# Turning the dilated heads two tokens at a time

## The chip, the core and the metric

The kernel runs on one NeuronCore of a Trainium2 chip. The metric is the device time of one execution in microseconds. Every execution starts with the inputs in HBM and ends when the last output tile has landed there.

The core has TensorE for matmuls (PE in the profile; PEld is its loading of weights), VectorE (DVE), ScalarE (ACT), GpSimd (POOL, which issues the loads here) and SyncE (SP, which issues the stores here). Each runs its own program in order and waits for the others on semaphores. Matmuls write PSUM; DVE and ACT copy results from there to SBUF.

## The reference

Sliding-window attention, of which half of the heads are dilated, and then a soft mixture of experts in which every expert sees four weighted means of all tokens.

```python
# q, k, v: (batch 8, heads 8, seq 576, head_dim 64), float32
scores = q @ k.T / 8
rel = pos[:, None] - pos[None, :]
mask_plain = (rel >= 0) & (rel < 32)                      # heads 0 to 3
mask_dil = (rel >= 0) & (rel < 128) & (rel % 4 == 0)      # heads 4 to 7
attn = softmax(where(mask, scores, -1e9));  out = attn @ v
x = out.transpose(0, 2, 1, 3).reshape(4608, 512)          # tokens x (heads * dim)

logits = x @ phi                                          # phi: 512 x 32 (8 experts x 4 slots)
d = softmax(logits over the 4608 tokens);   slot_input = d.T @ x
slot_out[e] = relu(slot_input[e] @ w1[e]) @ w2[e]         # w1[e]: 512x1024, w2[e]: 1024x512
c = softmax(logits over the 32 slots);      result = c @ slot_out   # 4608 x 512, float32
```

A dilated head sees, from a token, the 32 tokens before it with the same remainder mod 4. If the tokens are put in an order in which all of one remainder lie side by side, a dilated head has the same band of 32 as a plain one.

## The kernel before

**Units.** Attention is done in 8 units (`NU`). Unit u handles batches 2(u // 2) and 2(u // 2) + 1, and one type of heads, `ty = u % 2`: even units the four plain heads, odd units the four dilated ones. So a pair of units finishes two batches. `load_unit` (L387) brings q, k and v of a unit into one of three staging buffers `stg`, converted to bf16 by the DMA: 96 partitions (3 tensors x 2 heads `h01` x 8 pieces of 72 tokens x 2 batches `bpar`), and on the free axis two heads `x` x 72 tokens x 64 dims.

**Steps of a unit**, each an `op` with the engine that it runs on:

- `st_T` (turning; PE L515, ACT L532), four times, j = 0 to 3: PE transposes slices of `stg`, ACT copies them from PSUM to `TT`, where the head dims lie on the partitions. One transpose takes one token slot c of one head x: 96 partitions x 64 columns in, 64 x 96 out. The two heads x go to the partition halves 0 to 63 and 64 to 127. Each call makes 2 x 9 x 2 = 36 transposes. For odd units j is the remainder mod 4, so that `TT` holds the tokens in order of remainder.
- `st_S` (PE L550, ACT L557, DVE L565), six times: scores of four blocks of 96 queries against 128 keys (`QB` 96 plus a `HALO` of 32), for both partition halves; exp on ACT to `PT`; the mask times it on DVE.
- `st_V` (PE L575, DVE L580), four times: V turned back to tokens on partitions, with a column of ones: `VN`.
- `st_P` (PE L603, DVE L612 and L614), four times: P times V; division by the row sums gives `XB`, tokens on partitions.
- `st_X` (PE L631, then L640 on DVE or L641 on ACT), four times: `XB` turned by six transposes of 96 x 128, and one copy of 128 x 576 out of PSUM to `XT`. The planner gives a copy to DVE or to ACT, whichever is free first in its account.
- `st_L`, after each odd unit, for both of its batches: logits of a batch out of `XT` of the plain (c = 0, 1) and dilated heads (c = 2, 3), eight matmuls (PE L660); exp on ACT to `expT` (L665), in natural token order; two small copies `expX` (DVE L672); the logits turned to tokens on partitions, in the order of each head type (PE L692, DVE L696); and the sum over tokens of d.T @ x into `psA` (PE L705).

**Order.** All ops are handed to a planner in the kernel (`Prog.schedule`). Each has a cost, a due time (`due`, a `PACE` of 13.1 us a unit) and a mode of the PE array (`mode`: "f" full, "h" column halves, "r" row halves, "c" column quarters); a change of mode is booked at 0.11 us. The planner simulates the engines with these costs and writes the order of each engine's program; so a changed cost can change the order everywhere. From 125 us on in its own account it puts dummy matmuls (`filler`, L889) where it sees PE wait.

**Loads.** POOL issues all loads in program order. `load_unit(u + 3)` waits until unit u is turned, as it takes its staging buffer. The 16 weight matrices of the experts (1 MB each in bf16) go to a buffer of their own (`WD`, seven), into the staging buffers of units 5, 6 and 7 once those are turned (six), and into `TT` (three), once unit 7's scores and V are read.

**The end.** After unit 7: `fold` (L752), first layer (L772), row sums (L809), hidden layer turned (L790), second layer (L830), and then the output (L869, L872, L875, stores on SP).

Of the kernel before, what the change touches and what calls it, by code (L numbers as in the profile page):

```python
# [21 lines left out]
QB = 96  # L22
# [269 lines left out]
def bass_dilated_sliding_attn__then__soft_moe_slots_kernel(  # L292
# [205 lines left out]

    def win(u, t, h01, i, bpar):

        base = (2 * t + h01) * S + QB * i - (HALO if t else 0)
        n = QB if t == 0 else 128
        return TT[:, u % 2, 2 * base + bpar:2 * (base + n - 1) + bpar + 1:2]

    def st_T(u, j):
        ty, s = u % 2, u % 3
        src = stg[0:96, s, :].rearrange("r (x c d) -> r x c d", x=2, c=CT)
        pt = tile(psum, 2)

        def pe(t):  # L510
            for a in range(2):
                for kk in range(9):
                    c = 18 * j + 9 * a + kk if ty == 0 else 4 * (9 * a + kk) + j
                    for hx in range(2):
                        i_ = t.transpose(  # L515
                            bankb2(pt, a)[64 * hx:64 * hx + 64, 96 * kk:96 * kk + 96],
                            src[:, hx, c, :], ident[0:96, 0:96])
            return i_
        op("pe", pe, r=[b_id, b_stg[s]], w=[pt], alloc=[pt], cost=0.86, mode="h",
           key=due(u, 0.5 * j))  # L520

        def ev(ac):
            sv = pair(pt)[:, :, 0:432].rearrange("p a (k w) -> p w a k", w=48)
            t32 = TT[:, u % 2, :].bitcast(F32)
            if ty == 0:
                d = t32.rearrange("p (w c) -> p w c", c=CT)[:, :, 18 * j:18 * j + 18]
                d = d.rearrange("p w (a k) -> p w a k", a=2)
            else:
                d = t32.rearrange("p (s n) -> p s n", s=6)[:, :, 144 * j:144 * j + 144]
                d = d.rearrange("p s (w a k) -> p s w a k", a=2, k=9)  # L530
                sv = sv.rearrange("p (s w) a k -> p s w a k", w=8)
            return ac.activation(d, sv, ACTF.Copy)  # L532
        op("act", ev, r=[pt], **{"w" if j == 0 else "a": [b_TT[u % 2]]}, cost=0.8,
           key=due(u, 0.8 + 0.5 * j))
# [4 lines left out]
    def st_S(u, i):  # L539
        ty = u % 2  # L540
        sc, pt = tile(psum, 2), tile(pPT)
        U[u]["p", i] = pt

        def pe(t):
            for x in range(4):
                gi = 4 * i + x
                g, blk_ = gi // 6, gi % 6
                bpar, h01 = g // 2, g % 2
                for hx in range(2):
                    i_ = t.matmul(pair(sc)[:, hx, QB * x:QB * x + QB],  # L550
                                  win(u, 1, h01, blk_, bpar)[64 * hx:64 * hx + 64],
                                  win(u, 0, h01, blk_, bpar)[64 * hx:64 * hx + 64],
                                  start=True, stop=True)
            return i_
        k0 = due(u, 4.0 + 1.3 * i)
        op("pe", pe, r=[b_TT[u % 2]], w=[sc], alloc=[sc, pt], cost=0.2, mode="r", key=k0)
        op("act", lambda ac: ac.activation(  # L557
            sbt(pt)[:, 0:768].rearrange("p (x n) -> p x n", x=2), pair(sc)[:, :, 0:384],
            ACTF.Exp, scale=SCALE), r=[sc], w=[pt], cost=0.71, key=k0 + 0.6)
        m0 = (4 * i) % 6  # L560

        def mk(dv):
            m = mask[ty][:, m0:m0 + 4, :].rearrange("p m x -> p (m x)")
            p_ = sbt(pt)[:, 0:768].rearrange("p (x n) -> p x n", x=2)
            return dv.tensor_tensor(p_, p_, m.unsqueeze(1).to_broadcast([128, 2, 384]), AluOp.mult)  # L565
        op("dve", mk, r=[b_mask[ty]], w=[pt], cost=0.47, key=k0 + 1.5)
# [18 lines left out]
    def st_P(u, g):  # L585
        bp, ty = u // 2, u % 2
        bpar, h01 = g // 2, g % 2
        b = 2 * bp + bpar
        po, rv = tile(psum, 2), tile(pRV)
        vn = U[u]["v", g]  # L590
        al = [po]
        if h01 == 0:
            XB[b, ty] = tile(pXB)
            al.append(XB[b, ty])
        xb = XB[b, ty]
        pts = {(6 * g + m) // 4: U[u]["p", (6 * g + m) // 4] for m in range(6)}

        def pe(t):
            for m in range(6):
                i, x = divmod(6 * g + m, 4)  # L600
                for hx in range(2):
                    o_ = 384 * hx + QB * x
                    i_ = t.matmul(pair(po)[:, hx, 65 * m:65 * m + 65],  # L603
                                  sbt(pts[i])[:, o_:o_ + 128],
                                  sbt(vn)[:, m, hx, 0:65], start=True, stop=True)
            return i_
        k0 = due(u, 8.5 + 2.0 * g)
        op("pe", pe, r=list(pts.values()) + [vn], w=[po], alloc=al, cost=0.41, key=k0)

        def pv():  # L610
            return pair(po)[0:QB, :, 0:390].rearrange("p x (m d) -> p x m d", d=65)
        op("dve", lambda dv: dv.reciprocal(sbt(rv)[:], pv()[:, :, :, 64]),  # L612
           r=[po], w=[rv], alloc=[rv], cost=0.15, key=k0 + 1.0)
        op("dve", lambda dv: dv.tensor_tensor(  # L614
            sbt(xb)[:].rearrange("p m (x h d) -> p h x m d", x=2, h=2)[:, h01], pv()[:, :, :, 0:64],
            sbt(rv)[:].unsqueeze(3).to_broadcast([QB, 2, 6, 64]), AluOp.mult),
           r=[po, rv], **{"w" if h01 == 0 else "a": [xb]}, cost=0.87, key=k0 + 1.2)

    def st_X(u, bpar, x):
        bp, ty = u // 2, u % 2  # L620
        b = 2 * bp + bpar
        px = tile(psum, 1)
        al = [px]
        if x == 0:
            XT[b, ty] = tile(pXT)
            al.append(XT[b, ty])
        xt, xb = XT[b, ty], XB[b, ty]

        def pe(t):
            for m in range(6):  # L630
                i_ = t.transpose(bankb(px)[:, QB * m:QB * m + QB],  # L631
                                 sbt(xb)[:, m, 128 * x:128 * x + 128], ident[0:QB, 0:QB])
            return i_
        k0 = due(u, 13.0 + 4.0 * bpar + 0.8 * x)
        op("pe", pe, r=[b_id, xb], w=[px], alloc=al, cost=0.28, key=k0)

        def ev(en):
            d, s_ = sbt(xt)[:, x, :], bankb(px)[:, 0:S]
            if en is nc.vector:
                return en.tensor_copy(d, s_)  # L640
            return en.activation(d, s_, ACTF.Copy)  # L641
        op(("dve", "act"), ev, r=[px], **{"w" if x == 0 else "a": [xt]},
           cost={"dve": 0.38, "act": 0.55}, key=k0 + 0.6)

    def st_L(b, u):
        lg = tile(psum, 2)
# [2 lines left out]
        def pe(t):  # L649
            flat = pair(lg).rearrange("p a x -> p (a x)")  # L650
            for lo, hi in ((0, 192), (192, 576)):
                for c in range(4):
                    o_ = flat[:, 320 + lo:320 + hi]
                    if c < 2:
                        rhs = sbt(x0)[:, c, lo:hi]
                    else:
                        o_ = o_.rearrange("p (i r) -> p r i", r=4)
                        rhs = sbt(x1)[:, c - 2, :].rearrange("p (r i) -> p r i", r=4)[
                            :, :, lo // 4:hi // 4]
                    i_ = t.matmul(o_, phi_pad[:, c].rearrange("p j i -> p (j i)"), rhs,  # L660
                                  start=c == 0, stop=c == 3)
            return i_
# [5 lines left out]
            cost=0.56, key=k0 + 1.3)  # L668
        for h_ in range(2):
            def cp(dv, h_=h_):  # L670
                n = expT[:, S * b:S * b + S].rearrange("p (i x y) -> p x y i", x=2, y=2)
                return dv.tensor_copy(  # L672
                    expX[:].rearrange("p (x y i) -> p x y i", x=2, y=2)[:, :, h_],
                    n[:, :, h_, 96 * (1 - h_):96 * (1 - h_) + 48])
            op("dve", cp, r=[b_expT[b]], **{"w" if h_ == 0 else "a": [b_expX]}, cost=0.15,
               key=k0 + 2.2)
# [3 lines left out]
        def pe2(t):  # L680
            nat = expT[:, S * b:S * b + S]
            for i in range(12):
# [3 lines left out]
                elif m % 3 == 1:  # L686
                    l_ = expX[:, QB * (m // 3):QB * (m // 3) + QB]
                else:
                    f_ = QB * m
                    o_ = 4 * (f_ % 144) + f_ // 144  # L690
                    l_ = nat[:, o_:o_ + 4 * 95 + 1:4]
                i_ = t.matmul(bank(pe_t)[0:128 if i < 6 else QB, 32 * i:32 * i + 32], l_, sel[:],  # L692
                              start=True, stop=True)
            return i_
        op("pe", pe2, r=[b_expT[b], b_expX, b_sel] + b_expT[b + 1:b + 2], w=[pe_t], alloc=[pe_t, et], cost=0.5, key=k0 + 2.4)
        op("dve", lambda dv: dv.tensor_copy(  # L696
            sbt(et)[:], bank(pe_t)[0:QB, 0:384].rearrange("p (i s) -> p i s", s=32)),
           r=[pe_t], w=[et], cost=0.45, key=k0 + 3.2)
# [51 lines left out]
    def pe_f(t):  # L750
# [1 line left out]
            i_ = t.matmul(bank(fo)[:, 32 * c:32 * c + 32], psA_sb[:, c::4], fold[:],  # L752
                          start=True, stop=True)
        return i_
    op("pe", pe_f, r=[b_psA, b_fold], w=[fo], alloc=[fo], cost=1.4, key=K1)
    for hi in range(2):
        op("dve", lambda vv, hi=hi: vv.tensor_copy(
            siT[:, hi, :, :, 4 * hi:4 * hi + 4],
# [183 lines left out]
```

## Time and profile before

| | |
|---|---|
| runs | 640.96, 189.43, 189.08 us; median 189.43 |
| profiled execution | 190.36 us |
| its span, first to last instruction | 188.6 us |
| mean granted TensorE clock | 0.926 |
| PE busy | 142.1 us (75%), 2872 matmuls and as many weight loads |
| DVE, ACT busy | 110.1 us (58%), 94.2 us (50%) |
| loads (software queue) | 30.94 MB written to SBUF |
| stores | 9.44 MB to HBM |
| instruction queue (q8) | 22 packets, 0.36 MB |

How to read the rows of the profile: a row of the timeline is start and length in us, engine, line of the kernel, operation, output<-inputs, tile, and count of instructions that were merged; in brackets the idle time of the engine ahead of it and what ended it. `96*64 96x96` on PE: 96 rows and 64 columns of the array in use, 96 x 96 moving elements. "issue" as a releaser: the engine waited for nothing that the profile shows. A matmul's own length includes the way through the array; what a series costs is seen from start to start. In rows of groups, the numbers behind the bar are busy us, mean ns of one, then idle us ahead of them.

### The profile page before, as it was taken

Reading aid. Unit: us, or ns where it says so; the run is one execution under the profiler, and the core shown is the slowest. Engines: PE = TensorE matmul, PEld = TensorE weight load, DVE = VectorE, ACT = ScalarE, POOL = GpSimd, SP = SyncE. Lnnn points to the kernel's source line nnn. Section 1 sums busy time; section 2 is a strip of 40 time slices with the busy share of each in tenths; the row PEclk is TensorE's granted clock in tenths of the full one; section 3 lists DMA queues with packets and bytes.
Section 4 is the critical chain, followed back from the end, with each engine's and each line's share of the span. In section 5 each row is a group of like instructions: output and inputs, shape, how many; then the busy total and the mean of one; then the engine's idle time right before and its main releaser. Section 6 shows DMA issues by size and latency. Waiting matters only on the chain.

```text
span 188.6 us, 6342 instructions
## 1 busy us (share of the span) xinstructions
PE 142.1 (75%) x2872; PEld 104.4 (55%) x2872; DVE 110.1 (58%) x256; ACT 94.2 (50%) x136; POOL 35.8 (19%) x72
## 2 busy tenths in 40 slices
PE   0028879599987878998949799887899999996000
PEld 0028668487766757776837677675664658311000
DVE  6820794496687359569528966948943130699000
ACT  2006857456675655675649476478321020699000
POOL 7980603301500420440020020010400000000000
PEclk9999999669999978999996999999699999999855
DMA  5999999999999999999999999949999950199998
GB/s 76 211 215 211 213 212 218 213 216 215 212 210 220 216 208 221 213 212 215 216 216 208 219 219 217 208 99 151 219 215 214 215 109 3 60 405 405 407 403 322
DMA packets 7898, 40.83 MB, mean 216 GB/s; under 512 B 1856, under 2 KB 1856, under 8 KB 4416
## 3 DMA queue, kind: packets, MB, share of 16 engines
q0 software_dynamic: 4752, 30.94, 79.9%
q1 hardware_dynamic: 3120, 9.50, 12.8%
q8 instruction: 22, 0.36, 0.7%
q14 instruction: 4, 0.03, 0.0%
HBM read 61.93 MB, written 9.44 MB: 378 GB/s over the span
## 4 chain that ended last, share of the span: by engine, by line
PE 50%; DVE 26%; issue 5%; DMA 5%; ACT 4%; POOL 1%; DVEq 0%; POOLq 0%
PE ps L515 13%; DVE PT L565 8%; PE ps L660 6%; DVE XB L614 6%; PE ps L631 6%; DVE WD L875 5%; DVE VN L580 5%; DMA stg<-in_v_dram 5%; PE ps L889 4%; PE ps L575 4%; PE ps L603 3%; PE ps L550 3%; PE ps L830 3%; ACT PT L557 2%; PE ps L772 2%
## 5 line engine op out<-in xcount | busy, mean ns | idle before, releaser
L532 ACT ACTIVATE TT<-ps 128x864 f32<-128x864 f32 x32 | 28.3, 894 | 30.0 <-PE ps L515 30.0
L515 PE MATMUL ps<-ident,stg 96*64 96x96 bf16 x1152 | 32.4, 215 | 14.4 <-DMA stg<-in_v_dram 12.9
L557 ACT ACTIVATE PT<-ps 128x768 bf16<-128x768 f32 x48 | 37.4, 810 | 10.0 <-PE ps L550 10.0
L515 PEld LDWEIGHTS ps<-ident,stg 96*64 96x64 bf16 x1152 | 28.3, 116 | 16.6 <-DMA stg<-in_v_dram 12.9
L614 DVE TENSOR_TENSOR XB<-ps,RV 96x768 bf16<-96x768 f32 x32 | 30.2, 945 | 0.5
L580 DVE COPY VN<-ps 128x768 bf16<-128x768 bf16 x32 | 17.6, 549 | 19.2 <-PE ps L575 19.1
L550 PE MATMUL ps<-TT 64*128 64x96 bf16 x384 | 17.9, 221 | 4.5 <-issue 2.5
L603 PE MATMUL ps<-VN,PT 128*128 128x65 bf16 x384 | 19.0, 203 | 2.8 <-DVE VN L580 1.1
L575 PE MATMUL ps<-ident,TT 128*128 128x128 bf16 x192 | 18.4, 238 | 2.3 <-issue 2.3
L603 PEld LDWEIGHTS ps<-VN,PT 128*128 128x128 bf16 x384 | 15.7, 104 | 5.3 <-DVE VN L580 1.5
L396 POOL DMA_DIRECT2D stg<-in_q_dram x16 | 8.4, 526 | 51.3 <-PE ps L515 50.5
L631 PE MATMUL ps<-ident,XB 96*128 96x96 bf16 x192 | 13.6, 214 | 5.1 <-DVE XB L614 3.0
L575 PEld LDWEIGHTS ps<-ident,TT 128*128 128x128 bf16 x192 | 12.5, 107 | 7.9 <-issue 5.3
L631 PEld LDWEIGHTS ps<-ident,XB 96*128 96x128 bf16 x192 | 10.4, 103 | 8.1 <-issue 3.7
L550 PEld LDWEIGHTS ps<-TT 64*128 64x128 bf16 x384 | 10.8, 102 | 7.2 <-ACT PT L557 1.6
L641 ACT ACTIVATE XT<-ps 128x576 bf16<-128x576 bf16 x16 | 10.4, 648 | 8.2 <-PE ps L631 8.2
L640 DVE COPY XT<-ps 128x576 bf16<-128x576 bf16 x16 | 7.3, 455 | 11.4 <-PE ps L631 11.4
L565 DVE TENSOR_TENSOR PT<-PT,mask_d 128x768 bf16<-128x768 bf16 x24 | 12.8, 535 | 0.9 <-ACT PT L557 0.5
L660 PE MATMUL ps<-XT,phi_pad 128*128 128x192 bf16 (+1 forms) x64 | 13.0, 362 | 0.0
L565 DVE TENSOR_TENSOR PT<-PT,mask_p 128x768 bf16<-128x768 bf16 x24 | 12.7, 541 | 0.0
L612 DVE RECIPROCAL RV<-ps 96x12 f32<-96x12 f32 x32 | 7.1, 223 | 7.9 <-PE ps L603 7.8
L425 POOL DMA_DIRECT2D stg<-in_moe_w_dram x6 | 3.2, 534 | 42.1 <-PE ps L515 42.1
(75 smaller groups left out, 161.5 us busy)
## 6 DMA issues: line engine op xcount, KB each, us to landing
WD<-in_moe_w_dram POOLq DMA_DIRECT2D x7, 1024.0 KB, 25.4
out_dram<-WD SPq DMA_DIRECT2D x14, 512.0 KB, 5.0
stg<-in_moe_w_dram POOLq DMA_DIRECT2D x6, 1024.0 KB, 15.2
stg<-in_q_dram POOLq DMA_DIRECT2D x16, 288.0 KB, 13.2
stg<-in_k_dram POOLq DMA_DIRECT2D x16, 288.0 KB, 14.9
stg<-in_v_dram POOLq DMA_DIRECT2D x16, 288.0 KB, 17.5
TT<-in_moe_w_dram POOLq DMA_DIRECT2D x2, 1024.0 KB, 14.5
out_dram<-stg SPq DMA_DIRECT2D x4, 512.0 KB, 5.1
```

What stands on the lines that cost most here:

```text
L515: i_ = t.transpose(bankb2(pt, a)[64 * hx:64 * hx + 64, 96 * kk:96 * kk + 96], src[:, hx, c, :], ident[0:96, 0:96])
L532: return ac.activation(d, sv, ACTF.Copy)
L550: i_ = t.matmul(pair(sc)[:, hx, QB * x:QB * x + QB], win(u, 1, h01, blk_, bpar)[64 * hx:64 * hx + 64], win(u, 0, h01, blk_, bpar)[64 * hx: ...
L557: op("act", lambda ac: ac.activation(sbt(pt)[:, 0:768].rearrange("p (x n) -> p x n", x=2), pair(sc)[:, :, 0:384], ACTF.Exp, scale=SCALE), ...
L565: return dv.tensor_tensor(p_, p_, m.unsqueeze(1).to_broadcast([128, 2, 384]), AluOp.mult)
L575: i_ = t.transpose(bankb(pv)[:, 128 * m:128 * m + 128], win(u, 2, h01, m, bpar), ident[:, :])
L580: op("dve", lambda dv: dv.tensor_copy(sbt(vn)[:, :, :, 0:64], bankb(pv)[:, 0:768].rearrange("p (m x d) -> p m x d", m=6, x=2)), r=[pv], w= ...
L603: i_ = t.matmul(pair(po)[:, hx, 65 * m:65 * m + 65], sbt(pts[i])[:, o_:o_ + 128], sbt(vn)[:, m, hx, 0:65], start=True, stop=True)
L614: op("dve", lambda dv: dv.tensor_tensor(sbt(xb)[:].rearrange("p m (x h d) -> p h x m d", x=2, h=2)[:, h01], pv()[:, :, :, 0:64], sbt(rv)[: ...
L631: i_ = t.transpose(bankb(px)[:, QB * m:QB * m + QB], sbt(xb)[:, m, 128 * x:128 * x + 128], ident[0:QB, 0:QB])
L641: return en.activation(d, s_, ACTF.Copy)
L660: i_ = t.matmul(o_, phi_pad[:, c].rearrange("p j i -> p (j i)"), rhs, start=c == 0, stop=c == 3)
```

## The change

Odd units only, but for the costs:

- `st_T` transposes two neighbouring tokens of one head at once: 96 partitions x 128 columns in, 128 x 96 out, 18 transposes per call instead of 36. The even token of the two comes out on partitions 0 to 63 and the odd one on 64 to 127. The call's mode is "f" instead of "h". `TT` then holds, along its free axis, the two heads x one after the other, and in each of them the two remainders of one parity.
- The window `win` into `TT` and the place of a block in `st_P`'s PSUM tile follow; `XB` has its columns as before, its blocks in the order of parity, then remainder.
- `st_X` copies `XT` into natural token order while it leaves PSUM (read with a stride, written in order).
- `st_L` reads `XT` and writes PSUM in order; before, the dilated heads' matmuls wrote every fourth word. The `expX` copy and the slices of `pe2` (L692) follow the new block order.
- Costs that the planner reads: `st_T` 0.86 to 0.75 in odd units, `st_S` 0.20 to 0.22, `st_P` 0.41 to 0.46, `st_X` 0.28 to 0.31, its copy on DVE 0.38 to 0.80 in odd units and on ACT 0.55 to 0.57, `pe2` 0.50 to 0.56, fold 1.4 to 1.9.

```diff
     def win(u, t, h01, i, bpar):
-        base = (2 * t + h01) * S + QB * i - (HALO if t else 0)
+        if u % 2 == 0:
+            base = (2 * t + h01) * S + QB * i
+        else:
+            base = (6 * (i // 3) + 2 * t + h01) * 288 + QB * (i % 3)
+        base -= HALO if t else 0
...
     def st_T(u, j):
+        two = stg[0:96, s, :].rearrange("r (x c d) -> r x c d", x=2, d=128)
...
                 for kk in range(9):
-                    c = 18 * j + 9 * a + kk if ty == 0 else 4 * (9 * a + kk) + j
+                    if ty:
+                        c = 2 * (9 * a + kk) + j % 2
+                        i_ = t.transpose(bankb2(pt, a)[:, 96 * kk:96 * kk + 96],
+                                         two[:, j // 2, c, :], ident[0:96, 0:96])
+                        continue
+                    c = 18 * j + 9 * a + kk
                     for hx in range(2):
...
-        op("pe", pe, r=[b_id, b_stg[s]], w=[pt], alloc=[pt], cost=0.86, mode="h",
+        op("pe", pe, r=[b_id, b_stg[s]], w=[pt], alloc=[pt], cost=0.86 if ty == 0 else 0.75,
+           mode="h" if ty == 0 else "f",
...
-                d = t32.rearrange("p (s n) -> p s n", s=6)[:, :, 144 * j:144 * j + 144]
+                d = t32[:, 1728 * (j // 2):1728 * (j // 2) + 1728].rearrange(
+                    "p (s n) -> p s n", s=6)[:, :, 144 * (j % 2):144 * (j % 2) + 144]
...
     # st_P
+                    bk, po_ = (half, m) if ty == 0 else (m // 3, 3 * half + m % 3)
+                    i_ = t.matmul(pair(po)[:, bk, 65 * po_:65 * po_ + 65],
...
     # st_X
             d, s_ = sbt(xt)[:, x, :], bankb(px)[:, 0:S]
+            if ty:
+                s_ = s_.rearrange("p (y x s) -> p s x y", y=2, x=2)
+                d = d.rearrange("p (s x y) -> p s x y", y=2, x=2)
...
-           cost={"dve": 0.38, "act": 0.55}, key=k0 + 0.6)
+           cost={"dve": 0.38 if ty == 0 else 0.8, "act": 0.57}, key=k0 + 0.6)
...
     # st_L
-                    if c < 2:
-                        rhs = sbt(x0)[:, c, lo:hi]
-                    else:
-                        o_ = o_.rearrange("p (i r) -> p r i", r=4)
-                        rhs = sbt(x1)[:, c - 2, :].rearrange("p (r i) -> p r i", r=4)[
-                            :, :, lo // 4:hi // 4]
+                    rhs = sbt((x0, x1)[c // 2])[:, c % 2, lo:hi]
...
-                n = expT[:, S * b:S * b + S].rearrange("p (i x y) -> p x y i", x=2, y=2)
+                n = expT[:, S * b:S * b + S].rearrange("p (i y x) -> p x y i", x=2, y=2)
...
-                    f_ = QB * m
-                    o_ = 4 * (f_ % 144) + f_ // 144
+                    o_ = m // 3 + (4 * 48 + 2 if m % 3 else 0)
```

More of the change, by code (lines that the diff above doesn't have):

```diff
@@ L555, in st_S @@
         k0 = due(u, 4.0 + 1.3 * i)
-        op("pe", pe, r=[b_TT[u % 2]], w=[sc], alloc=[sc, pt], cost=0.2, mode="r", key=k0)
+        op("pe", pe, r=[b_TT[u % 2]], w=[sc], alloc=[sc, pt], cost=0.22, mode="r", key=k0)
         op("act", lambda ac: ac.activation(
@@ L600, in pe @@
                 i, x = divmod(6 * g + m, 4)
-                for hx in range(2):
-                    o_ = 384 * hx + QB * x
-                    i_ = t.matmul(pair(po)[:, hx, 65 * m:65 * m + 65],
+                for half in range(2):
+                    o_ = 384 * half + QB * x
+                    bk, po_ = (half, m) if ty == 0 else (m // 3, 3 * half + m % 3)
+                    i_ = t.matmul(pair(po)[:, bk, 65 * po_:65 * po_ + 65],
                                   sbt(pts[i])[:, o_:o_ + 128],
-                                  sbt(vn)[:, m, hx, 0:65], start=True, stop=True)
+                                  sbt(vn)[:, m, half, 0:65], start=True, stop=True)
             return i_
         k0 = due(u, 8.5 + 2.0 * g)
-        op("pe", pe, r=list(pts.values()) + [vn], w=[po], alloc=al, cost=0.41, key=k0)
+        op("pe", pe, r=list(pts.values()) + [vn], w=[po], alloc=al, cost=0.46, key=k0)
         def pv():
@@ L634, in st_X @@
         k0 = due(u, 13.0 + 4.0 * bpar + 0.8 * x)
-        op("pe", pe, r=[b_id, xb], w=[px], alloc=al, cost=0.28, key=k0)
+        op("pe", pe, r=[b_id, xb], w=[px], alloc=al, cost=0.31, key=k0)
         def ev(en):
             d, s_ = sbt(xt)[:, x, :], bankb(px)[:, 0:S]
+            if ty:
+                s_ = s_.rearrange("p (y x s) -> p s x y", y=2, x=2)
+                d = d.rearrange("p (s x y) -> p s x y", y=2, x=2)
             if en is nc.vector:
@@ L694, in pe2 @@
             return i_
-        op("pe", pe2, r=[b_expT[b], b_expX, b_sel] + b_expT[b + 1:b + 2], w=[pe_t], alloc=[pe_t, et], cost=0.5, key=k0 + 2.4)
+        op("pe", pe2, r=[b_expT[b], b_expX, b_sel] + b_expT[b + 1:b + 2], w=[pe_t], alloc=[pe_t, et], cost=0.56, key=k0 + 2.4)
         op("dve", lambda dv: dv.tensor_copy(
@@ L754, in pe_f @@
         return i_
-    op("pe", pe_f, r=[b_psA, b_fold], w=[fo], alloc=[fo], cost=1.4, key=K1)
+    op("pe", pe_f, r=[b_psA, b_fold], w=[fo], alloc=[fo], cost=1.9, key=K1)
     for hi in range(2):
```

## The prediction

> **What bounds the kernel now.** I read the page first: the slices, then the queues, then the chain that ended last.
>
> ```profile
> span 188.6 us, 6342 instructions
> PE 142.1 (75%) x2872; PEld 104.4 (55%) x2872; DVE 110.1 (58%) x256; ACT 94.2 (50%) x136; POOL 35.8 (19%) x72
> GB/s 76 211 215 211 213 212 218 213 216 215 212 210 220 216 208 221 213 212 215 216 216 208 219 219 217 208 99 151 219 215 214 215 109 3 60 405 405 407 403 322
> q8 instruction: 22, 0.36, 0.7%
> PE 50%; DVE 26%; issue 5%; DMA 5%; ACT 4%; POOL 1%; DVEq 0%; POOLq 0%
> ```
>
> A slice is 188.6/40 = 4.715 us. From slice 1 to 25 the DMA moves about 214 GB/s without a dip: the loads are at their limit there. But in slices 26 and 27 they fall to 99 and 151, a loss of (115 + 63)/214 x 4.715 = **3.9 us**, and they end in slice 32, long before the kernel does. So the loads are a floor, and today something else sits above it. The chain names PE for half of the span, and 5% "issue": PE waiting for nothing that the profile shows. I looked at those places in the timeline of PE.
>
> ```profile
> 61.30 0.74 PE L515 MATMUL ps<-ident,stg 96*64 96x96 bf16 x26 [0.90 <-issue]
> 61.98 0.56 PE L603 MATMUL ps<-VN,PT 128*128 128x65 bf16 x12
> 62.46 1.72 PE L515 MATMUL ps<-ident,stg 96*64 96x96 bf16 x72
> 64.11 0.43 PE L631 MATMUL ps<-ident,XB 96*128 96x96 bf16 x6
> 64.48 0.35 PE L550 MATMUL ps<-TT 64*128 64x96 bf16 x8
> 64.75 0.34 PE L575 MATMUL ps<-ident,TT 128*128 128x128 bf16 x3
> 67.43 0.33 PE L575 MATMUL ps<-ident,TT 128*128 128x128 bf16 x3 [2.33 <-issue]
> 67.60 0.42 PE L631 MATMUL ps<-ident,XB 96*128 96x96 bf16 x6
> ...
> 35.09 0.56 PE L631 MATMUL ps<-ident,XB 96*128 96x96 bf16 x5 [2.14 <-issue]
> ...
> 98.48 0.20 PE L550 MATMUL ps<-TT 64*128 64x96 bf16 x1 [2.52 <-issue]
> ```
>
> PE stops in the middle of a series of six transposes that have one common wait ahead of the first: no semaphore can be the cause. Between the end of the stop at 61.30 and the next stop it ran 26 + 12 + 72 + 6 + 8 + 3 = 127 matmuls, each with its weight load. The instruction queue moved 0.36 MB in 22 packets, 16 KB each. Next: the DMA view of the two stretches between the long stops, and the busy times there.
>
> ```profile
> q8 instruction: 5, 0.08, 0.9%
> q8 instruction: 5, 0.08, 1.0%
> ```
> ```profile
> 35.09:67.43 32.34, 27.91 (x636) 22.45 (x636) 20.69 (x44) 19.87 (x28) 7.09 (x14) 0.90 1.03 215
> 67.43:98.48 31.05, 26.80 (x636) 21.59 (x636) 21.58 (x46) 19.09 (x27) 5.16 (x10) 0.95 1.03 214
> 98.48:126.30 27.82, 25.70 (x591) 20.47 (x590) 20.64 (x45) 18.29 (x26) 1.06 (x2) 0.94 0.97 203
> 67.50:72.00 4.50, 4.50 (x76) 3.52 (x76) 3.96 (x9) 3.55 (x6) 0.00 (x0) 0.64 1.01 212
> ```
>
> The columns behind the length are PE, PEld, DVE, ACT, POOL, then clock, DMA share, GB/s. Each stretch is one pair of units (an even one and an odd one): 636 matmuls, 636 weight loads and five packets of instructions, so 127 matmuls a packet, the very count between two stops. PE stops where a packet of its program ends and the next isn't there. Where one stop follows a packet behind another (61.30 to 67.43), a packet took **6.13 us** with a saturated DMA; five are 30.7 us, and the pair took 31.05. No engine is that full: PE was busy 26.80, of which 4.50 at a clock of 0.64 after the stop (at full clock 2.9, so 25.2 in all), DVE 21.58, ACT 19.09. **So I take the fetching of PE's program as what paces the attention phase.**
>
> **The change part by part.**
>
> *Turning odd units.* st_T issued 36 transposes of 64 columns, now 18 of 128, four times in each of four odd units: 288 matmuls and 288 weight loads fewer, 72 of each per pair. PE's own time first.
>
> ```profile
> 59.64 0.43 PE L631 MATMUL ps<-ident,XB 96*128 96x96 bf16 x6
> ...
> 74.98 0.68 PE L631 MATMUL ps<-ident,XB 96*128 96x96 bf16 x12 [0.68 <-DVE XB L614]
> 75.59 0.96 PE L515 MATMUL ps<-ident,stg 96*64 96x96 bf16 x36
> ```
>
> Narrow: (1.72 - 0.96)/36 = 21 ns each, as two run side by side on the column halves. Wide: L631 has exactly the new shape, and (0.68 - 0.43)/6 = 42 ns. 36 x 21 and 18 x 42 are the same 0.76 us. What goes is the change of array layout: from three L575 at 67.43 to L631 at 67.60 is 0.17 (3 x 56 ns, nothing between), but from six L631 at 64.11 (6 x 42 = 0.25) to L550 at 64.48 is 0.37, so 0.1 us is lost at a change. Three of four blocks of an odd unit stand between full-width neighbours (L631, L603, L660) and save two changes: 3 x 0.2 = 0.6 a unit.
>
> The program: 564 instead of 636 matmuls a pair are 4.43 packets, 4.43 x 6.13 = **27.2 us instead of 30.7**. That stays above the work of each engine, so the fetch still paces. Four odd units save at most 4 x 0.567 x 6.13 = 13.9 us by the last turning; I take 12, since packets without the dense turning hold more work each and will wait more on DVE.
>
> [...]
>
> *Logits.* Odd heads wrote PSUM four words apart; now all eight matmuls write in order.
>
> ```profile
> 137.37 1.62 PE L660 MATMUL ps<-XT,phi_pad 128*128 128x192 bf16 x8
> 138.79 0.72 PE L631 MATMUL ps<-ident,XB 96*128 96x96 bf16 x12
> 139.34 0.81 PE L889 MATMUL ps<-mask_p,ident 128*128 128x512 bf16 x3
> ...
> 142.79 1.04 PE L889 MATMUL ps<-mask_p,ident 128*128 128x512 bf16 x4
> ```
>
> The eight take 138.79 - 137.37 = 1.42 us. In order, a 512-column matmul costs about 1.04 - 0.81 = 0.23 (0.42 to 0.45 ns a column); 4 x 192 + 4 x 384 = 2304 columns are then 0.97 to 1.04. Saved: 0.4 each, 3.2 over eight batches, but only the last two (0.8) lie behind the last turning, outside the fetch's pace.
>
> *Copies of XT.* The 16 copies of odd units now read PSUM 144 and 288 elements apart.
>
> ```profile
> L641 ACT ACTIVATE XT<-ps 128x576 bf16<-128x576 bf16 x16 | 10.4, 648 | 8.2 <-PE ps L631 8.2
> L640 DVE COPY XT<-ps 128x576 bf16<-128x576 bf16 x16 | 7.3, 455 | 11.4 <-PE ps L631 11.4
> L532 ACT ACTIVATE TT<-ps 128x864 f32<-128x864 f32 x32 | 28.3, 894 | 30.0 <-PE ps L515 30.0
> L614 DVE TENSOR_TENSOR XB<-ps,RV 96x768 bf16<-96x768 f32 x32 | 30.2, 945 | 0.5
> ```
>
> ACT: L532 already reads PSUM 48 words apart at 1.03 ns an element, against 1.13 for L641, so nothing to pay. DVE: 0.79 ns an element today; L614, with spaced reads of four bytes, pays 1.23, so 576 of them are at most 0.71 us. No row has two-byte reads this far apart on DVE; the bounds are 0 and +0.25, and I take +0.25. If half fall to DVE, that is 8 x 0.25 = 2 us, 0.5 a pair: 22.1 of 27.2, hidden. Without that cover it would cost the 2 us.
>
> *The rest* (windows into TT, P's bank, the expX copy, the slices of pe2) keeps count and shape of each instruction: zero. The TT copy keeps its 864 elements. No DMA and no wait is added. The planner's changed costs write a new order that I can't read from this trace: 0 to a few us either way, in the range.
>
> **The end.** Twelve us earlier can't all be kept.
>
> ```profile
> 126.62 1.06 POOL L425 DMA_DIRECT2D stg<-in_moe_w_dram  x2 [15.65 <-PE ps L515]
> 133.00 2.12 POOL L425 DMA_DIRECT2D TT<-in_moe_w_dram  x4 [5.32 <-PE ps L550]
> TT<-in_moe_w_dram POOLq DMA_DIRECT2D x1, 256.0 KB, 20.5
> ```
> ```profile
> 159.62 1.85 PE ps L830 x16
> 161.47 0.75 PE ps L889 x3
> 162.23 0.45 PE ps L869 x2
> 162.70 9.31 DVE WD L875 x14
> ```
>
> The weights for the staging buffer wait for the last turning (126.62); with 12 us less they are queued at about 115, before the DMA runs dry at 122.6, and the 3.9 us hole closes. The last piece, issued about 134.6 and landed 20.5 later at 155.1, then lands at **151.2**. Behind it stand four matmuls of expert 7 (a quarter of 1.85, plus 0.2 for the semaphore): L830 ends no sooner than 151.9, against 161.47 today: **-9.6**. PE's own path gives 161.47 - 12 - 0.8, plus about 1 as its program is still fetched through a full queue: 149.7, below that floor. From 161.47 on nothing changes: the output runs at 405 GB/s.
>
> **Sum.** -9.6 + 0.6 for a landing that PE doesn't meet exactly = -9.0. Profiled execution: 190.36 us (span 188.6 and 1.8 around it), so 181.4; the median of the runs is 189.43, 0.9 lower: **180.4**.
>
> **Rivals.**
> (a) *The waits move.* With the fetch loosened, DVE's order takes over (26% of the chain is DVE). If a pair falls only to 29.5, four odd units save some 6 us, the hole closes half, and L830 ends near 156: -5.5, **184**. For it: packets without the dense turning hold more passes of DVE each. Against: DVE has 5 us of room a pair.
> (b) *The stops aren't fetches*, or fetching fewer packets is no faster. Then PE's saving alone counts: 3.2 + 4 x 0.6, less the 2 us of DVE copies: -3.6, **186**. [...] Against it: 127 matmuls a packet and between stops.
> (c) *The copy out of PSUM bites.* L660 waits for the copies, and the turnings and scores of the next unit are queued behind it on PE. A copy of 2 us (3.5 ns an element) adds 1.5 on 16 copies; two thirds exposed are 16, **196**. It ends above 193.2 from 13 us exposed beyond the forecast. Against: 1.03 ns on L532's spaced reads.
> (d) *The edit doesn't make fewer instructions:* the loops show 18 for 36; I give it nothing.
>
> **Chances.** Forecast 0.60 (179.0 to 182.5), (a) 0.18, (b) 0.13, (c) 0.09. A measurement of this kernel tells about 2% (3.8 us) from no change. Faster than 185.6: 0.60 and most of (a) = 0.74; within: (b) and the rest = 0.17; slower 0.09. The range reaches from 179.0, just under the floor of 179.8, over (a) and most of (b) to 187.0.
>
> **What would show it.** Right: PE and PEld 288 fewer each (fewer or more L889 apart); about 20 instruction packets; long "issue" stops gone or short; pairs near 27 to 28 us; slices 26 and 27 at 214 GB/s; the last L830 soon behind the last landing near 151; L660 about 1.0 us; DVE copies in two kinds, 455 and about 700. Wrong: stops of 2 us with 127 matmuls between, at the old places; DVE XB or XT ahead of PE's waits in each pair; a copy over 1 us.

## The result, and the profile after

The changed kernel takes **182.34 us** (median of 4 runs, 181.55 to 183.92) where the kernel before, on the same chips, takes 190.22: a ratio of **0.9615, interval 0.9505 to 0.9726**. Its profiled execution took 182.96 us, with a span of 181.2. Forecast were 180.4 us against 189.43, a ratio of 0.952. A second timing of the changed kernel, made later beside two variants of it, gave a median of 181.65 us and 0.9524 (0.9478 to 0.9569). Some executions of several versions take over 1.5% longer than the fastest of the same version (one of `c_all_old_order` took 185.28 us at a mean granted clock of 0.897, the other five 181.41 to 182.77 at 0.936 to 0.960): the ratios here leave them out, the medians don't.

The profile's page of the changed kernel, the lines that answer to those of before:

```profile
span 181.2 us, 5750 instructions
PE 133.0 (73%) x2579; PEld 98.6 (54%) x2584; DVE 113.0 (62%) x257; ACT 92.9 (51%) x135; POOL 35.8 (20%) x72
GB/s 78 201 216 209 215 217 213 214 213 213 213 217 215 217 211 214 216 210 224 205 221 208 221 210 224 210 224 208 217 217 213 217 171 29 145 406 405 405 403 319
q8 instruction: 20, 0.33, 0.7%
PE 29%; DMA 24%; DVE 23%; ACT 7%; POOL 6%; issue 3%; DVEq 0%; POOLq 0%
```

The dip in slices 26 and 27 is gone: the loads run at some 214 GB/s from slice 1 to slice 31 without a break. Two packets of instructions fewer were fetched. The chain that ended last is no longer half PE; 24% of it is DMA: 14% is the wait for weights in `TT`, and 10% the first loads of the kernel. The row of the wait, from the chain:

```profile
121.30 26.05 DMA TT<-in_moe_w_dram
```

So the end has changed hands, from PE to the loads.

Busy times in two pairs of units, each from the first slot matmul of a pair (L705, now L715) to that of the next (columns as before: PE, PEld, DVE, ACT, POOL, clock, DMA share, GB/s). First the kernel before:

```profile
51.69:83.57 31.88, 27.05 (x642) 21.83 (x642) 21.73 (x46) 19.79 (x28) 7.64 (x15) 0.95 1.03 215
83.57:115.24 31.67, 27.10 (x642) 21.69 (x641) 21.48 (x46) 19.97 (x28) 2.12 (x4) 0.95 1.03 215
```

and the changed one:

```profile
47.70:75.86 28.16, 24.61 (x569) 20.19 (x568) 22.26 (x47) 19.75 (x28) 7.62 (x15) 1.00 1.03 215
75.86:103.52 27.66, 24.68 (x569) 20.24 (x568) 22.18 (x47) 19.64 (x28) 2.14 (x4) 1.00 1.03 215
```

73 matmuls fewer in a pair, and 3.7 and 4.0 us less. Forecast were 27.2 as the floor of the fetch, and 27 to 28. The timeline of PE shows what is left of its stops between 20 and 120 us, all four in the middle of a series:

```profile
42.59 0.87 PE L525 MATMUL ps<-ident,stg 96*64 96x96 bf16 x31 [0.37 <-issue]
67.58 0.83 PE L525 MATMUL ps<-ident,stg 96*64 96x96 bf16 x29 [0.17 <-issue]
73.99 0.26 PE L562 MATMUL ps<-TT 64*128 64x96 bf16 x4 [1.12 <-issue]
98.67 0.61 PE L525 MATMUL ps<-ident,stg 96*64 96x96 bf16 x19 [0.27 <-issue]
```

1.9 us in all, where before four took 7.9 (the three long ones 7.0). The profile of the second timing has six, 4.5 us in all, the longest 1.60. And the issues on POOL, of the first profile, with the landing of the last piece from the view of the DMA:

```profile
114.39 1.07 POOL L425 DMA_DIRECT2D stg<-in_moe_w_dram  x2 [13.74 <-PE ps L520]
120.78 2.12 POOL L425 DMA_DIRECT2D TT<-in_moe_w_dram  x4 [5.33 <-PE ps L562]
```
```profile
TT<-in_moe_w_dram POOLq DMA_DIRECT2D x1, 256.0 KB, 30.0
```

The last turning is over 12.2 us sooner (126.62 to 114.39; the forecast took 12), in the profile of the second timing 9.8 (116.78). The last piece is issued about 122.4 and lands at 152.4 instead of 155.1.

### The profile page after: what moved, and what is told of

Its sections match the earlier page's. It is cut to its first block, busy times and chain, and to the rows that moved or that the text cites. A ratio compares the mean times of both kernels' runs of the same rounds, so it can differ in the third digit from the quotient of the medians.

```text
span 181.2 us, 5750 instructions
## 1 busy us (share of the span) xinstructions
PE 133.0 (73%) x2579; PEld 98.6 (54%) x2584; DVE 113.0 (62%) x257; ACT 92.9 (51%) x135; POOL 35.8 (20%) x72
## 4 chain that ended last, share of the span: by engine, by line
PE 29%; DMA 24%; DVE 23%; ACT 7%; POOL 6%; issue 3%; DVEq 0%; POOLq 0%
DMA TT<-in_moe_w_dram 14%; DMA stg<-in_v_dram 10%; DVE XB L627 6%; DVE PT L577 5%; DVE WD L885 5%; PE ps L525 5%; ACT PT L569 4%; POOL stg L396 4%; PE ps L587 4%; PE ps L671 3%; PE ps L520 3%; DVE VN L592 3%; PE ps L840 3%; PE ps L644 3%; PE ps L562 3%
## 5 line engine op out<-in xcount | busy, mean ns | idle before, releaser
L544 ACT ACTIVATE TT<-ps 128x864 f32<-128x864 f32 x32 | 28.5, 893 | 30.5 <-PE ps L525 21.6
L525 PE MATMUL ps<-ident,stg 96*64 96x96 bf16 x576 | 17.7, 222 | 16.3 <-DMA stg<-in_v_dram 13.5
L525 PEld LDWEIGHTS ps<-ident,stg 96*64 96x64 bf16 x576 | 15.4, 121 | 18.1 <-DMA stg<-in_v_dram 13.6
L592 DVE COPY VN<-ps 128x768 bf16<-128x768 bf16 x32 | 17.5, 548 | 10.1 <-PE ps L587 9.9
L562 PE MATMUL ps<-TT 64*128 64x96 bf16 x384 | 15.2, 204 | 3.1 <-issue 1.1
L587 PE MATMUL ps<-ident,TT 128*128 128x128 bf16 x192 | 16.3, 221 | 0.7 <-DVE VN L592 0.5
L656 DVE COPY XT<-ps 128x576 bf16<-128x576 bf16 x17 | 10.1, 597 | 9.7 <-PE ps L644 9.6
L644 PE MATMUL ps<-ident,XB 96*128 96x96 bf16 x192 | 12.8, 208 | 3.6 <-DVE XB L627 3.6
L520 PE MATMUL ps<-ident,stg 96*128 96x96 bf16 x288 | 14.9, 206 | 0.1
L587 PEld LDWEIGHTS ps<-ident,TT 128*128 128x128 bf16 x192 | 10.9, 98 | 4.6 <-issue 1.5
L562 PEld LDWEIGHTS ps<-TT 64*128 64x128 bf16 x384 | 9.6, 94 | 6.8 <-issue 1.2
L520 PEld LDWEIGHTS ps<-ident,stg 96*128 96x128 bf16 x288 | 13.0, 98 | 0.3 <-ACT PT L569 0.3
L644 PEld LDWEIGHTS ps<-ident,XB 96*128 96x128 bf16 x192 | 9.6, 98 | 5.5 <-DVE XB L627 4.4
L879 PE MATMUL ps<-so_sb,expT 128*128 128x512 bf16 x35 | 10.3, 384 | 0.9 <-DVE WD L885 0.3
## 6 DMA issues: line engine op xcount, KB each, us to landing
WD<-in_moe_w_dram POOLq DMA_DIRECT2D x7, 1024.0 KB, 28.4
```

The source lines that it names most:

```text
L520: i_ = t.transpose(bankb2(pt, a)[:, 96 * kk:96 * kk + 96], two[:, j // 2, c, :], ident[0:96, 0:96])
L525: i_ = t.transpose(bankb2(pt, a)[64 * hx:64 * hx + 64, 96 * kk:96 * kk + 96], src[:, hx, c, :], ident[0:96, 0:96])
L562: i_ = t.matmul(pair(sc)[:, hx, QB * x:QB * x + QB], win(u, 1, h01, blk_, bpar)[64 * hx:64 * hx + 64], win(u, 0, h01, blk_, bpar)[64 * hx: ...
L587: i_ = t.transpose(bankb(pv)[:, 128 * m:128 * m + 128], win(u, 2, h01, m, bpar), ident[:, :])
L592: op("dve", lambda dv: dv.tensor_copy(sbt(vn)[:, :, :, 0:64], bankb(pv)[:, 0:768].rearrange("p (m x d) -> p m x d", m=6, x=2)), r=[pv], w= ...
L644: i_ = t.transpose(bankb(px)[:, QB * m:QB * m + QB], sbt(xb)[:, m, 128 * x:128 * x + 128], ident[0:QB, 0:QB])
```

## The experiments

Two theories stood against each other. **Fetch**: PE's program arrives at a packet of about 127 matmuls per 6 us while the DMA is full, and fewer instructions mean fewer packets. **PE time**: what counts is how long PE itself is at work, and the stops have another cause.

**One half of the change at a time.** All three versions here keep the planner's costs and modes of before, so that the order of the work is that of before. `a_turn_only` is the wide turning; XT is copied as it lies, and the dilated logits are still written with a stride:

```diff
 # st_X: no change of order in the copy; st_L:
+  o_ = o_.rearrange("p (s x y) -> p y x s", x=2, y=2)
+  rhs = sbt(x1)[:, c - 2, :].rearrange("p (y x s) -> p y x s", y=2, x=2)[:, :, :, lo // 4:hi // 4]
```

> The wide turning alone, in the order of before: 18 transposes of 128 columns for 36 of 64 in odd units; XT is copied in the order of parity as it lies, and the dilated heads' logits still write every fourth word. Fetch theory (the fetching of PE's program paces the attention): 576 PE instructions fewer, about 20 instruction packets, a pair of units falls from 31.7 to about 28 us, the time by 6 to 8 us to about 182 to 184. PE-time theory (PE's own seconds are what counts): only the changes of array layout are saved, 4 x 0.6 = 2.4 us, time about 187.

Measured: ratio **0.9564 (0.9454 to 0.9674)**, median of all six 185.10 us. The ratio rests on two of the six times, 181.60 and 183.55; the other four are 184.61 to 186.48, and the profile is of the longest. Its two pairs:

```profile
51.65:80.06 28.41, 25.56 (x571) 20.55 (x570) 21.76 (x46) 19.65 (x28) 7.63 (x15) 1.00 1.03 215
80.06:111.38 31.32, 28.49 (x571) 22.86 (x570) 21.62 (x46) 19.65 (x28) 2.12 (x4) 0.89 1.03 215
```

20 packets of instructions were fetched, and the stops between 20 and 120 us come to 2.6 us. The pair at full clock took 28.4 us, as forecast. The other took 31.3, though it has but one stop, of 0.23 us: 6.8 us of it ran at half clock (its mean is 0.89), behind a wait of 0.92 us for `XB` (the last section comes back to this).

`b_copy_logits` is the other half: the turning stays narrow.

```diff
+  s_ = s_.rearrange("p (r s) -> p s r", r=4);  d = d.rearrange("p (s r) -> p s r", r=4)   # st_X, odd units
-  o_ = o_.rearrange("p (i r) -> p r i", r=4)   # st_L, and rhs likewise
+  rhs = sbt((x0, x1)[c // 2])[:, c % 2, lo:hi]
```

> The other half alone, in the order of before: narrow turning kept, XT put in natural order by the copy, logits read and written in order. Fetch theory: 22 packets, the long stops at the old places, a pair still 31 to 32 us although PE has 0.8 us less to do in it; only the last two logits count, time 188.5 to 190. PE-time theory: 8 x 0.4 = 3.2 us less, time about 186 to 187. In both, L660 from start to next start falls from 1.42 to about 1.0 us, and a DVE copy with stride takes 0.70 to 0.75 us.

Measured: ratio **0.9951 (0.9908 to 0.9993)**, median 189.91 us. It fetched 22 packets, and logits took 0.99 us. The windows of its two pairs, and its long stops in the timeline:

```profile
51.12:82.86 31.74, 26.09 (x641) 21.40 (x641) 22.33 (x47) 19.97 (x28) 7.65 (x15) 0.95 1.03 215
82.86:114.78 31.92, 26.29 (x641) 21.42 (x640) 21.96 (x47) 19.96 (x28) 2.12 (x4) 0.95 1.03 214
```
```profile
35.40 0.56 PE L631 MATMUL ps<-ident,XB 96*128 96x96 bf16 x5 [2.70 <-issue]
67.28 0.33 PE L575 MATMUL ps<-ident,TT 128*128 128x128 bf16 x3 [2.60 <-issue]
98.56 0.20 PE L550 MATMUL ps<-TT 64*128 64x96 bf16 x1 [2.52 <-issue]
```

This is the plainest of the pairs of theories: PE has 0.8 to 1.0 us less to do in a pair, and the pair is as long as before. What PE saved came back as stops. The one at 35 us grew from 2.14 to 2.70 at the same matmul, the one at 67 from 2.33 to 2.60, and two shorter ones came up (0.34 and 0.90): 10.1 us between 20 and 120, against 7.9 before. With the DMA full, PE's own time does not set the pace.

`c_all_old_order` is the whole change with the costs and modes of before:

```diff
-  cost=0.86 if ty == 0 else 0.75, mode="h" if ty == 0 else "f"
+  cost=0.86, mode="h"            # and the other costs as before
```

> The whole change with the planner's costs and modes of before, so in the order of before. If the new order is no part of the gain: 181.5 to 183.5, as the changed kernel. If the new order carries part of it, 184 or more.

Measured: 181.64 us, ratio **0.9522 (0.9461 to 0.9583)**. The new order is no measurable part of the gain in time. Its pairs took 30.34 us (clock 0.89) and 28.54, more than the changed kernel's; but its last second layer ends at 152.61, no later than the changed kernel's (154.05 and 152.88 in its two profiles), so the time doesn't show it.

**Instructions without work.** `f_after_dummy`: if packets are what counts, then as many instructions as the turning saved, with next to no work in them, must bring the time back.

```diff
 # pe2 (L692 of before), after its twelve matmuls
+  for i in range(36):
+      t.matmul(bank(pe_t)[32 * (i % 4):32 * (i % 4) + 32, 400:401], sel[:], nat[:, 0:1], start=True, stop=True)
```

> The changed kernel with 36 tiny matmuls added to each batch's L692 block (32 columns, one moving element, four side by side on the column quarters, result unused): 288 matmuls and 288 weight loads more, as many instructions as the turning had taken out, but hardly any work; order unchanged. Fetch theory: 22 packets again, pairs of units back from 28 to 30.7 us or more, the last turning some 9 us later, time 187 to 191. PE-time theory: 72 x about 10 ns and four layout changes are some 1.1 us a pair, most of it under the floor of the loads: 182 to 184.5.

Measured: **190.46 us, 0.9884 (0.9802 to 0.9966)** of the kernel before, against 0.9615 and 0.9524 in the two timings without the dummies. It fetched 22 packets. The dummies and the matmul behind them in the timeline, and the windows of the pairs:

```profile
85.37 0.42 PE L705 MATMUL ps<-expT,sel 128*32 128x1 bf16 x36
85.72 0.84 PE L616 MATMUL ps<-VN,PT 128*128 128x65 bf16 x12
```
```profile
49.91:82.06 32.15, 26.92 (x642) 22.33 (x641) 22.41 (x46) 19.39 (x28) 7.67 (x15) 0.95 1.02 213
82.06:113.19 31.13, 27.89 (x641) 22.99 (x640) 22.52 (x46) 19.63 (x28) 2.11 (x4) 0.89 1.03 216
```

36 dummies take 85.72 - 85.37 = 0.35 us, 0.7 a pair; the pairs grew by 4.0 and 3.5, in part by stretches of lower clock (0.95 and 0.89). Eleven stops, 8.7 us in all, stand between 20 and 120 us.

**The other side: a DMA with nothing to do.** If it is the loads (some 214 GB/s) that hold the packets up, then with the loads cut away the same program should be fetched in time. `e_after_light` is the changed kernel so, `h_after_light_dummy` has the dummies too, and `d2_before_light` is the kernel before.

```diff
 # load_unit: units 3 to 7 bring 64 of 4608 columns;  wload: all matrices but w1[0] bring 64 columns
+  n = 4608 if u < 3 else 64
+  g.dma_start(d_[:, lo_:lo_ + 1, 0:64], v_[:, lo_:lo_ + 1, 0:64])
```

> The changed kernel with the loads of units 3 to 7 and of all weight matrices but one cut to slivers (old data and one matrix stand for the rest), so that the DMA is nearly idle from about 30 us until the output; order unchanged. Fetch theory: a packet comes in about 4 us instead of 6.1, pairs fall from 27.9 to 25.5 to 27.5 us, no stop at a packet's end. If the pace is set by PE and DVE alone: pairs stay at 27.7 to 28.2.

> Both edits together: tiny matmuls added, loads cut to slivers. Fetch theory: against the run with light loads alone the pairs grow only by PE's own cost, 0.5 to 1.5 us, not by 3, since packets come in time. PE-time theory: the same growth as with full loads.

> The kernel before with the same light loads, now including the second-layer matrices, so that the DMA is idle to the end of attention. Fetch theory: no stop of 2 us after 35 us; pairs of 28 to 28.6 us where the clock isn't cut (the earlier light run gave 28.5 and, with 6.8 us at half clock, 31.6). If fetching isn't the cause: 31.7 and the stops at the old places.

The windows of a pair, first the changed kernel with light loads, then the same with the dummies, then the kernel before with light loads (the next pair of each took 26.90, 27.37 and 28.50):

```profile
47.08:73.98 26.90, 24.24 (x570) 20.07 (x570) 22.21 (x47) 19.64 (x28) 7.40 (x15) 1.00 0.07 7
```
```profile
47.33:74.69 27.36, 25.09 (x641) 20.82 (x640) 22.23 (x47) 19.64 (x28) 7.65 (x15) 1.00 0.06 6
```
```profile
51.48:79.95 28.47, 25.78 (x641) 20.73 (x641) 21.70 (x46) 19.53 (x28) 7.65 (x15) 1.00 0.07 7
```

The DMA is idle (share 0.05 to 0.07) and PE shows no idle time put down to "issue" in any of these windows. The one stop that is left in the kernel before, 2.10 us, ends at 35.31, ahead of these windows. DVE and ACT are busy for nearly as long as with full loads (21.6 and 19.5 us a pair in the kernel before, against 21.6 and 19.9), so here the loads cost DVE nothing and ACT some 0.3 us a pair. As times, the three take 176.62, 178.61 and 184.06 us; they have most of their loads missing and are comparable among themselves only. The dummies cost 0.5 us a pair now, and 2.0 us over the whole, against 3.7 a pair and, by the ratios, 5 to 7 us with full loads. So 3.2 of the 3.7 us a pair that these instructions cost are there only with the DMA full (the stretches of lower clock among them), and I put them down to the fetch. The kernel before, with light loads, does a pair in 28.5 instead of 31.8 with PE's program unchanged: by the same reckoning 3.3 us a pair were the fetch (with the half clock behind a long stop in it: the mean clock of a pair is 0.95 with full loads and 1.00 with light ones). The changed kernel has only 27.9 - 26.9 = 1.0 left of this. And 28.5 - 26.9 = 1.6 is what the two programs differ by in their own work and order; PE's busy time falls by as much (25.78 to 24.24). By this reckoning, of the 3.9 us that a pair fell with full loads, 2.3 are the fetch and 1.6 are PE's shorter work: the fetch is the larger part, not the whole.

A first attempt at light loads, `d_before_light`, kept the second-layer matrices whole, so that the DMA was idle from about 37 to 95 us only.

> The kernel before with the loads of units 3 to 7 and of seven first-layer weight matrices cut to slivers (attention then works on old data, and one matrix stands for eight), so that the DMA is nearly idle after 30 us; program and order of all engines are those of before. Fetch theory: instruction packets come sooner after they are asked for, no stop of 2 us is left, and a pair takes 25 to 28 us. If the stops have a cause on PE itself: three stops over 2 us as before, pairs of 31 to 32 us.

Measured: the stops at 61, 67 and 98 us are gone, the one at 35 us, just as the loads ended (218 and 211 GB/s in the slices up to 32.3 us, 68 in the one to 36.9), has stayed at 1.9 us. But both pairs missed the expected 25 to 28 us, one by 0.5 and one by 3.6:

```profile
50.88:82.45 31.57, 28.88 (x641) 22.89 (x641) 21.70 (x46) 19.55 (x28) 7.62 (x15) 0.89 0.07 6
82.45:110.95 28.50, 25.82 (x642) 20.71 (x642) 21.55 (x46) 19.54 (x28) 2.11 (x4) 1.00 0.54 102
```

The same program: at a mean clock of 0.89 a pair takes 31.57 and at 1.00 28.50, and the longer pair is the one with the idler DMA. A wait for XB came before the stretch of half clock; the later run with all loads light has the same wait and kept its clock. The row in the one, and in the other:

```profile
70.78 0.68 PE L634 MATMUL ps<-ident,XB 96*128 96x96 bf16 x12 [0.92 <-DVE XB L617]
```
```profile
71.37 0.68 PE L634 MATMUL ps<-ident,XB 96*128 96x96 bf16 x12 [0.92 <-DVE XB L617]
```

**The end.** The profile of the changed kernel has dummy matmuls ahead of the last expert's second layer (the chain of waits, below). Left out:

```diff
-  if gap > 0.4 and n > 0:
+  if gap > 0.4 and n > 0 and o.key < 1009.0:
```

> The changed kernel without the nine dummy matmuls that the planner put around the last expert's second layer (six ahead of it and three behind); all else and all orders as they are. Reading of the profile: five of them stand, 1.24 us long, between the landing of the second to last piece and the matmuls that need only that piece; without them twelve of the sixteen run before the last piece lands. End of L840 about 1.1 us sooner, time 1 us below the changed kernel. If the end hangs on the last landing alone: no change.

> The whole change in the order of before, without the dummies around the last expert's second layer: 0 to 1.2 us below the same without that edit (181.6), 180.5 to 181.6.

> The changed kernel itself, on the same chip as the two versions without the last dummies: 181.5 to 183.

Measured: 181.60 us (ratio 0.9515, 0.9479 to 0.9550), 181.76 (0.9524, 0.9487 to 0.9561), and 181.65 for the changed kernel beside them (0.9524, 0.9478 to 0.9569). No difference, so both expectations of a gain missed. My reading that the dummies cost 1 us fits single executions: in the profile of `g_after_nofill`, where the matmuls ahead of the last sixteen also ran at the pace of half clock (three in 0.21 us, as in the first profile of the changed kernel at a clock of 0.50), the sixteen end at 152.75 (150.81 + 1.94), 1.3 us sooner than in the first profile of the changed kernel. As a rule it is wrong. No version beat the changed kernel.

## Why the prediction was right, and where it was off

**The pace.** That a packet of instructions takes some 6.1 us behind a full DMA, and that this paced the attention, is shown from four sides: fewer instructions and nearly the same PE seconds (`a_turn_only`), fewer PE seconds and the same instructions (`b_copy_logits`), instructions without work (`f_after_dummy`), and the fetch without the loads (the three versions with light loads). The traces hold a fifth, the time of each packet of the instruction queue. Before the change, packets end at 33.75, 59.93, 66.02 and 97.04 us, and the four stops of PE end at 35.09, 61.30, 67.43 and 98.48, each 1.35 to 1.43 later. In the first profile of the changed kernel packets end at 41.02, 66.34, 72.61 and 97.34 us, and its four stops end 1.2 to 1.6 us later. With the DMA full, between 20 and 120 us, no packet follows the one before it by less than 5.92 us before the change and 5.80 after it; where the loads fell to 99 GB/s before the change (slice 26), one followed after 4.07 (122.74 to 126.82).

One thing the prediction had too broad: five packets at 6.13 us each as the floor of a pair. Packets follow each other after 5.9 to 6.8 us before the change (from 27.5 to 116.3 us), and PE stops only at four of them; at the others no stop shows. And pairs of 27 to 28 us don't speak for a floor of 27.2 alone, as the changed kernel takes 26.9 with light loads, where no stop is put down to "issue".

Rival (b) of the prediction is out: PE's program before the change had four stops, 7.9 us in all, with the DMA full, and with light loads (`d2_before_light`) none after 35.31 us. Rival (a), DVE's order, did not take over: pairs took 27.7 and 28.2, not 29.5. But it shows: in the two pairs of the changed kernel PE's waits for DVE and ACT come to some 4.4 us, those put down to "issue" to 1.5.

**The turning.** In the timeline a wide block and what stands around it:

```profile
84.08 0.42 PE L644 MATMUL ps<-ident,XB 96*128 96x96 bf16 x6
84.34 0.93 PE L520 MATMUL ps<-ident,stg 96*128 96x96 bf16 x18
85.10 0.55 PE L616 MATMUL ps<-VN,PT 128*128 128x65 bf16 x12
```

18 transposes from start to next start: 0.76 us, the 18 x 42 ns of the working, and nothing is lost between neighbours of the same layout (six L644 in 0.26).

**Logits and copies.** Two rows of PE, two of the copies:

```profile
99.21 1.16 PE L671 MATMUL ps<-XT,phi_pad 128*128 128x192 bf16 x8
100.20 0.42 PE L644 MATMUL ps<-ident,XB 96*128 96x96 bf16 x6
```
```profile
71.73 0.76 DVE L656 COPY XT<-ps 128x576 bf16<-128x576 bf16 x1 [1.02 <-PE ps L644]
72.81 0.65 ACT L657 ACTIVATE XT<-ps 128x576 bf16<-128x576 bf16 x1
```

Logits 0.99 us instead of 1.42, as worked out. ACT pays nothing for the stride (0.65; its mean was 648 ns before and is 650 now). DVE's copy grew from 0.455 to 0.76, by 0.30; I had set 0.25 as the upper bound, so the bound from L614 was too low by 0.05. It is hidden (pairs of 28.16 and 27.66 us with it, 28.41 at full clock without it in `a_turn_only`), and rival (c), which reckoned with copies of 2 us, is out.

**The size of the end** is the term that was off. The span fell by 7.4, not 9.0. The chain of waits of the changed kernel, its last pieces:

```profile
147.39 3.42 PE ps L840 x38
150.80 0.16 issue
150.96 1.24 PE ps L899 x5
152.20 1.85 PE ps L840 x16
```

L840 ends at 154.05, where the prediction had 151.9 as the floor and 152.5 with its 0.6 for a missed landing. Two steps of "The end" failed. First, the landing: 152.4, not 151.2. I had taken the 3.9 us hole as the whole gain of the loads, as if they ended as before. The DMA view of the last 4 us ahead of the landing, before (151.1 to 155.1) and after (148.4 to 152.4):

```profile
q0 software_dynamic: 193, 0.47, 60.1%
```
```profile
q0 software_dynamic: 102, 0.24, 30.6%
```

The stream thins out at its end in both, but after the change it thins out more: 0.23 MB less in the last 4 us, which is 1.1 us at 214 GB/s, and the landing is 1.2 late. What thins it the runs do not show. Second, only four matmuls behind the landing: in the profiled execution all sixteen stood there, from 152.2 on, with five dummies ahead of them, as the 38 ahead of them ran at half clock after PE had waited 2.91 us for weights. The row and the windows:

```profile
147.39 0.40 PE L840 MATMUL ps<-stg,hT 128*32 128x256 bf16 x1 [2.91 <-DMA TT<-in_moe_w_dram]
```
```profile
141.00:147.20 6.20, 3.43 (x76) 2.38 (x76) 0.77 (x3) 0.45 (x2) 0.00 (x0) 0.99 1.02 212
147.20:150.50 3.30, 3.11 (x45) 2.26 (x48) 0.00 (x0) 0.00 (x0) 0.00 (x0) 0.50 0.66 130
```

In the profile of the second timing, with a span of 180.1, the chain has the sixteen end at 152.88. The row, and the issue and landing of the last piece:

```profile
150.96 1.92 PE ps L840 x16
```
```profile
123.17 2.12 POOL L425 DMA_DIRECT2D TT<-in_moe_w_dram  x4 [5.33 <-PE ps L562]
```
```profile
TT<-in_moe_w_dram POOLq DMA_DIRECT2D x1, 256.0 KB, 27.5
```

There the last piece is issued at about 124.8 and lands 27.5 us later, at 152.3 again, though it was issued 2.4 us later than in the first profile: the loads, and not the attention, set the end, as forecast. Here the step of four matmuls behind the landing held, 152.88 against 152.3. The 0.2 us that it had for the semaphore stand in no row: in this profile PE starts 0.04 us behind the landing of the piece before (150.92 to 150.96). Of the 1.25 us from the forecast of 180.4 to this timing's 181.65, 1.1 are the landing.

## What to carry to other kernels

Where an engine stops in the middle of a series that has no wait of its own, count its instructions from stop to stop and the packets of the instruction queue in the same stretch: if they agree, and the DMA is full, suspect that the engine waits for its program, and compare with an idle DMA. Here it was the number of instructions that had to fall first, more than the seconds: 72 matmuls a pair fewer took a pair from 31.9 to 28.4 us (`a_turn_only`, its pair at full clock), 0.8 to 1.0 us of PE's work less left it at 31.7 and 31.9 (`b_copy_logits`). So two half-width matmuls side by side were no bargain: 36 of them and 18 wide ones take the same 0.76 us. And before the gain is claimed in full, look for the next floor: here the last turning came 12.2 us sooner and the end 7.4 in one profile, 9.8 and 8.5 in the other.

## What the runs showed that I had not expected

Half clock is a second price, behind some waits and not behind others. In two profiles of one attention program with an idle DMA, the same wait of 0.92 us was followed once by half clock (a pair of 31.57 us, clock 0.89) and once not (28.47, clock 1.00). `a_turn_only` and `c_all_old_order`, both in the order of before, have the same wait in each of their two pairs: in one pair the twelve transposes behind it take 1.11 us (at 99.77 and at 68.07) and the pair has a clock of 0.89, in the other they take 0.68 and 0.69, at 1.00.

Before the change, half clock was granted from 34.60 to 41.42 us, from 68.73 to 72.14 and from 99.45 to 102.86, and all these edges lie whole multiples of 3.41 us apart. On this grid, the stretch that the wait fell in and the one behind it, first in the run that lost its clock and then in the one that kept it:

```profile
67.98:71.39 3.41, 2.11 (x60) 1.81 (x60) 3.38 (x8) 1.08 (x3) 0.00 (x0) 1.00 0.02 5
71.39:74.80 3.41, 3.41 (x78) 3.20 (x77) 1.73 (x4) 1.40 (x2) 0.00 (x0) 0.50 0.00 0
```
```profile
69.98:73.39 3.41, 2.49 (x84) 2.16 (x80) 2.79 (x6) 1.96 (x3) 0.00 (x0) 1.00 0.02 5
73.39:76.81 3.42, 3.42 (x69) 2.65 (x68) 1.76 (x4) 2.28 (x5) 2.20 (x5) 1.00 0.06 7
```

PE was at work for 2.11 us of the one stretch, which half clock followed, and for 2.49 of the other, which it didn't. Whether the busy time of the stretch decides is not shown.

The three long stops for instructions before the change each had a stretch of half clock behind them (a mean of 0.64 from 67.5 to 72); in the changed kernel the clock stayed at 1.00 in both of the pairs shown.
